# An attention and MoE kernel on one core: the order of its instructions taken from a table in place of a list scheduler

## The chip, the core and the metric

The kernel runs on one core of a Trainium2 chip. The metric is device time in microseconds (us) of one execution. The engines are named as in the profile: PE is TensorE, PEld its weight loads, DVE is VectorE, ACT ScalarE, POOL GpSimd and SP SyncE, which issues nearly all DMAs. Each engine works through its own list of instructions in the order in which the program emits them and waits on semaphores for the others.

## The reference

The inputs are q, k and v of 4 batches, 8 heads, 576 positions and 64 elements a head, a memory per head (M_prev, z_prev), a gate per head and four MoE weights. All is fp32.

```python
scores = scale * np.matmul(q, k.transpose(0, 1, 3, 2))       # causal mask, softmax over keys
local = np.matmul(a, v)
q_p = phi(q)                                                 # elu(q) + 1
mem_out = (q_p @ M_prev) / (q_p @ z_prev + 1e-06)            # per head
attn = g * mem_out + (1 - g) * local                         # g = sigmoid(beta)
x = attn.transpose(0, 2, 1, 3).reshape(2304, 512)
h = np.maximum(np.maximum(x @ w1, x @ w2), x @ w3)           # 512 -> 768
out = h @ w_out                                              # 768 -> 512
```

## The kernel before

**Tiling.** The 576 positions are cut in two halves of 320 and 256 (HALVES). The work of attention is done in 32 pairs: half by half, batch by batch, two heads at a time (`pairs`). For one pair the kernel loads q, k and v, builds phi(q) on ACT, DVE and POOL, brings q and k into transposed form, takes the scores (`scores_top`, `scores_both`, `scores`: bank bs), masks them and takes the row minimum on DVE, the exponential on ACT and the scaling on POOL. The scaled phi(q) lies in the same buffer p as the probabilities, so that one product with [M_prev; v] gives the gated sum (`values`: bank bv). P is transposed on PE (bank bt) for pairs 0 to 9, and from pair 10 by DVE and two DMAs (`turn_h`, `turn_p`, `move_h`, `move_p`, tiles dh, dp and pt). The result goes as a high and a low part (xh, xl) into SBUF.

**MoE.** When the four pairs of a batch and half are done, their x is one group of 320 or 256 rows; there are eight groups. A group has 18 pieces of 12 matmuls (`moe_up`: 4 slices of 128 inputs, 3 products of high and low parts each, fp32r) and two or three of 18 or 36 (`moe_down`), all in the banks bm. The slices of one piece need the x of one pair each, so the first three matmuls of group 0 can run when pair 0 is done and the last three when pair 3 is. Until all weights are in, the pieces have only bank bm0, for the other two serve the decoding of weights: 24 chunks, each loaded by SP, widened by ACT and DVE and split by ACT and POOL or DVE (`load_weights`); six chunks are decoded early, then one with each piece.

**The plan.** Nothing is emitted while this program runs. `Plan` (L94) notes each operation with its regions of SBUF and PSUM and so with what it depends on (`note`). A copy may have two forms, ACT or DVE, and a subtraction of a low part two, DVE or POOL (`copy`, `combine`). `emit` starts from ranks in order of noting, some of them set later (`P.late`), and shakes them with 156 seeds (`shaken`). `run` (L353) then is a list scheduler with costs per operation, delays between engines (`AFTER`), 250 ns more for a PE instruction that waits for another engine (`SLACK`) and a simple model of DMA; it picks the form that ends first and emits the ready operation of lowest rank on the engine that is free first. For a change between PE's tile shapes (128 by 128, 64 rows, 64 columns) it adds time. All planned instructions are emitted on one line, L452.

**Fillers.** Until the first operation that writes bank bm0, `run` emits on PE a matmul of zeros into bm0 (L416) wherever its plan has a gap. These are the fillers:

```python
if e == "pe" and filler:
    while when - free[e] > (FILL_GAP if free[e] < WARM else FILL_WARM):
        if real:
            self.nc.tensor.matmul(**filler)
        free[e] += 107 if free[e] < WARM else 54
```

Of the kernel before, what the change touches and what calls it, by code (L numbers as in the profile page):

```python
# [12 lines left out]
F32 = mybir.dt.float32  # L13
# [12 lines left out]
class Half:  # L26

# [24 lines left out]

FILL_GAP, FILL_WARM, FILL_FROM, WARM = 60, 80, 450, 7500


NEAR = 1

SEEDS = (
# [18 lines left out]
)  # L82

BANK = (((0, 512),),)


class Op:
    __slots__ = (
        "eng", "cost", "fn", "args", "prio", "num", "deps", "users", "left", "move", "at", "end", "can",
        "more",  # L90
    )


class Plan:  # L94

    ENGINES = {"pe": "tensor", "dve": "vector", "act": "scalar", "pool": "gpsimd", "sp": "sync"}

    AFTER = {
        "pe": {"pe": 0, "dve": 200, "act": 200, "pool": 200, "sp": 190},
        "dve": {"pe": 235, "dve": 130, "act": 130, "pool": 205, "sp": 120},
        "act": {"pe": 200, "dve": 145, "act": 130, "pool": 160, "sp": 145},
        "pool": {"pe": 200, "dve": 115, "act": 220, "pool": 100, "sp": 70},
        "sp": {"pe": 2800, "dve": 2800, "act": 2800, "pool": 2800, "sp": 2800},
    }  # L110


    PEN = {"dve": 300}

    SLACK = 250

    def __init__(self, nc):
        self.nc = nc
        self.ops = []
        self.seen = {}  # L120
        self.filler = None
        self.kept = set()
        self.tied = []
        self.late = 0

    @staticmethod
    def region(ap):

        if ap.space == bass.MemoryType.DRAM:
            last = sum(st * (n - 1) for st, n in ap.ap)  # L130
            return 0, 1, ((ap.offset, ap.offset + last + 1),)
        row = ap.ap[0][0]
        dims = sorted(
            ((abs(st), n) for st, n in ap.ap[1:] if n > 1 and st and st % row), reverse=True
        )
        p0, f0 = divmod(ap.offset, row)
        p1 = p0 + ap.ap[0][1] + sum(st // row * (n - 1) for st, n in ap.ap[1:] if st % row == 0)
        size = 1
        while dims and dims[-1][0] <= max(size, 4):
            st, n = dims.pop()  # L140
            size += (n - 1) * st
        runs = [f0]
        for st, n in dims:
            runs = [r + i * st for r in runs for i in range(n)]
        return p0, p1, tuple((r, r + size) for r in runs)

    @staticmethod
    def meet(a, b):
        return (
            a[0] < b[1] and b[0] < a[1]  # L150
            and any(r0 < t1 and t0 < r1 for r0, r1 in a[2] for t0, t1 in b[2])
        )

    @staticmethod
    def covers(a, b):
        return (
            a[0] <= b[0] and b[1] <= a[1]
            and all(any(r0 <= t0 and t1 <= r1 for r0, r1 in a[2]) for t0, t1 in b[2])
        )
# [25 lines left out]
    def cost(self, eng, name, kw):  # L185
        out = kw["out"]
        n = 1
        for d in out.shape[1:]:
            n *= d
        if name == "dma_start":  # L190
            return {80: 680, 64: 715}.get(out.shape[0], 510)
        if eng == "pe":
            if name == "transpose":
                return 2.5 + 0.837 * kw["in_"].shape[0]
            if kw["rhs"].dtype != F32:
                return 13.3 + n / 2.4
            if self.mode(name, kw)[0] == 64:
                return 106 + 1.67 * n if out.shape[0] > 64 else 115
            return 1.69 * n
        psum = any(  # L200
            isinstance(a, bass.AP) and a.space == PSUM for a in kw.values()
        )
        if eng == "dve":
            if name == "reciprocal":
                return 75 + 6.25 * max(0, n - 1)
            if name in ("tensor_scalar", "tensor_copy") and not psum:
                return 68 + 0.52 * n
            if name == "tensor_reduce":
                n = 1
                for d in kw["in_"].shape[1:]:  # L210
                    n *= d
            if name == "tensor_tensor_reduce":
                return 76 + 1.042 * n + 62 * isinstance(kw["scalar"], bass.AP)
            return 68 + 1.042 * n
        if eng == "act":
            c = (51 if psum else 93) + 0.833 * n
            if out.space == PSUM:
                c += 80
            if len(out.shape) == 3 and out.ap[-1][0] > 1 and psum:
                c += 190  # L220
            return c + 93 * sum(isinstance(kw.get(a), bass.AP) for a in ("bias", "accum_out"))
        if eng == "pool":
            if name == "tensor_tensor":
                a = kw["in0"]
                apart = out.offset // out.ap[0][0] != a.offset // a.ap[0][0]
                return 142 + 2.13 * n + 140 * apart
            if name == "tensor_scalar":
                return 310 + 0.87 * n
            return 100 + 1.1 * n
        raise ValueError(eng)  # L230

    @staticmethod
    def mode(name, kw):

        w = kw["in_" if name == "transpose" else "lhsT"]
        rows = 64 if w.shape[0] <= 64 else 128
        if name == "transpose" or w.dtype != F32:
            return rows, 128
        return rows, 64 if w.shape[-1] <= 64 else 128

    @staticmethod
    def move(*aps):

        piece, size = 4096, 4
        for d in aps[0].shape:
            size *= d
        for ap in aps:
            run = 4
            for st, n in reversed(ap.ap if ap.space == bass.MemoryType.DRAM else ap.ap[1:]):
                if 4 * st != run:  # L250
                    break
                run *= n
            piece = min(piece, run)
        many = any(st == 0 for ap in aps for st, n in ap.ap[:1])
        if aps[0].shape[0] == 32 and piece > 1024:
            return size / piece * (31 + 0.0475 * piece) / 16
        return size / piece * (125 if many else 9.7 + 0.0435 * piece) / 16

    @classmethod
    def tiling(cls, eng, name, kw):  # L260

        if eng != "pe":
            return None, None, 0
        w = kw["in_" if name == "transpose" else "lhsT"]
        mode = cls.mode(name, kw)
        if mode == (128, 64):
            return mode, kw["out"].offset // kw["out"].ap[0][0] // 64, 0
        return mode, w.offset // w.ap[0][0] // 64, w.shape[-1]

    @staticmethod  # L270
    def shares(eng, name, kw):

        if eng == "pool":
            return True
        if eng != "dve":
            return False
        aps = [a for a in kw.values() if isinstance(a, bass.AP) and a.shape[-1] > 1]
        inputs = [a for k, a in kw.items() if k in ("in_", "in0", "in1") and a.space != PSUM]
        if len(inputs) > 1:
            return True  # L280
# [5 lines left out]
    def note(self, can):  # L286
# [12 lines left out]
        if after is not None:  # L299
            ins += after if isinstance(after, list) else [after]  # L300
# [1139 lines left out]
```

## Time and profile before

| | us |
|---|---|
| median of 3 runs | 481.31 (481.14 to 483.03) |
| profiled execution, first to last instruction | 478.1 (its whole time is not given apart from this) |
| PE busy | 468.6 |
| DVE, POOL, ACT busy | 345.0, 296.8, 279.7 |

The busy time of an engine is the time covered by its instructions. Matmuls are pipelined and overlap, so their durations are longer than the distance from one start to the next; where a cost is read, the starts are compared. The profile shows an fp32 matmul of less than the full array as two instructions. In the rows below "x" is a count, and in square brackets stands the idle time of the engine before an instruction and what ended it.

### The profile page before, as it was taken

The page shows a single profiled execution, that of the slowest core. Times are in us where ns is not written, and L with a number is a line of the kernel's source. Part 1 is how long each engine was busy: PE and PEld are TensorE (multiplying, and loading weights), DVE is VectorE, ACT ScalarE, POOL GpSimd, SP SyncE. Part 2 cuts the span into 40 slices and gives each one's busy share as a digit, 9 for nine tenths or more (in the row PEclk, how much of TensorE's full clock was granted, in tenths as well). Part 3 has the DMA queues.
Part 4 walks back from the last instruction along what each step waited for, and adds up shares of the span by engine and source line. Part 5 has one row for each costly group of instructions (what it writes and reads, how often), then busy time and mean ns, then how long its engine had stood idle before and what let it go on. Part 6 is the DMA issues. An engine that isn't in the chain of part 4 may idle for free.

```text
span 478.1 us, 10593 instructions
## 1 busy us (share of the span) xinstructions
PE 468.6 (98%) x3387; PEld 407.7 (85%) x3387; DVE 345.0 (72%) x1127; ACT 279.7 (59%) x784; POOL 296.8 (62%) x452
## 2 busy tenths in 40 slices
PE   9989999999999999999999999999999999999996
PEld 7654778787999889998999888997999888988995
DVE  3788999997689967687688766887779676630230
ACT  5588987886668563565556655746566565422111
POOL 3866797977878866476558864876776776511000
PEclk9998999999999999999999999999999999999999
DMA  5788888765558978777999999999997887674001
GB/s 124 179 221 262 231 223 241 235 164 127 128 122 220 252 172 224 176 185 232 262 215 236 258 260 252 239 209 260 267 268 201 219 244 198 198 198 111 23 0 46
DMA packets 147256, 94.24 MB, mean 197 GB/s; under 512 B 99968, under 2 KB 126848, under 8 KB 147200
## 3 DMA queue, kind: packets, MB, share of 16 engines
q1 hardware_dynamic: 146384, 93.36, 74.4%
q8 instruction: 27, 0.44, 0.4%
q10 hardware_dynamic: 816, 0.20, 0.2%
q14 instruction: 29, 0.24, 0.2%
HBM read 61.94 MB, written 31.59 MB: 196 GB/s over the span
## 4 chain that ended last, share of the span: by engine, by line
PE 91%; DMA 4%; SPq 2%; ACT 1%; issue 0%; DVE 0%; ACTq 0%
PE bm L452 64%; PE bv L452 11%; PE bs L452 10%; PE bt L452 4%; DMA rw<-in_moe_w_dram 4%; PE bm L416 2%; SPq L452 2%; DMA rk<-in_q_dram 1%; ACT p L452 0%; ACT k L452 0%; ACT rk L452 0%; ACT t L452 0%; DVE bm L452 0%; DVE p L452 0%; ACT bm L452 0%
## 5 line engine op out<-in xcount | busy, mean ns | idle before, releaser
L452 PE MATMUL bm<-xh,wh 128*128 128x320 f32 (+1 forms) x576 | 170.6, 302 | 0.5 <-DVE xh L452 0.3
L452 PE MATMUL bm<-xl,wh 128*128 128x320 f32 (+1 forms) x576 | 169.3, 299 | 0.0
L452 PE MATMUL bm<-xh,wl 128*128 128x320 f32 (+1 forms) x576 | 168.0, 297 | 0.0
L452 POOL TENSOR_SCALAR p<-p,sum,gb 128x320 f32<-128x320 f32 (+3 forms) x128 | 89.4, 703 | 38.8 <-DVE sum L452 27.0
L452 PEld LDWEIGHTS bm<-xh,wh 128*128 128x128 f32 x576 | 108.1, 190 | 3.6 <-ACT t L452 0.9
L452 PEld LDWEIGHTS bm<-xl,wh 128*128 128x128 f32 x576 | 108.6, 190 | 1.2 <-issue 0.3
L452 PEld LDWEIGHTS bm<-xh,wl 128*128 128x128 f32 x576 | 108.4, 189 | 1.2 <-issue 0.8
L452 ACT ACTIVATE p<-p,st 128x320 f32<-128x320 f32 (+4 forms) x144 | 84.2, 585 | 42.2 <-DVE st L452 39.9
L452 DVE TENSOR_TENSOR t<-bm,t 128x320 f32<-128x320 f32 (+1 forms) x96 | 43.1, 449 | 49.6 <-PE bm L452 42.0
L452 DVE CUSTOM_DVE_ANT_0 p<-bs,mask 128x320 f32<-128x320 f32 (+3 forms) x128 | 59.1, 470 | 15.3 <-PE bs L452 14.9
L452 PE MATMUL bs<-k,qs 128*128 128x288 f32 (+5 forms) x264 | 59.4, 311 | 0.0
L452 DVE STREAM_TRANSPOSE rk<-p 128x512 f32<-128x512 f32 (+1 forms) x80 | 55.7, 720 | 2.4 <-POOL p L452 2.1
L452 POOL TENSOR_TENSOR p<-phf,nn 128x128 f32<-128x128 f32 (+1 forms) x96 | 37.4, 396 | 15.6 <-DVE rk L452 6.9
L452 PEld LDWEIGHTS bs<-k,qs 128*128 128x128 f32 (+1 forms) x264 | 42.0, 186 | 3.6 <-issue 1.7
L452 PE MATMUL bv<-pt,rv 128*64 128x256 f32 (+1 forms) x384 | 42.9, 348 | 0.0
L452 POOL TENSOR_TENSOR xl<-kt,xh 128x256 fp32r<-128x256 f32 (+1 forms) x28 | 22.6, 808 | 31.9 <-ACT kt L452 31.3
L452 PEld LDWEIGHTS bv<-pt,rv 128*64 128x64 f32 x384 | 29.4, 139 | 15.2 <-issue 0.8
L452 PE MATMUL bm<-woh,hl 128*128 128x512 f32 (+1 forms) x102 | 39.0, 384 | 0.0
L452 PE MATMUL bm<-woh,hh 128*128 128x512 f32 (+1 forms) x102 | 38.8, 384 | 0.0
L452 PE MATMUL bm<-wol,hh 128*128 128x512 f32 (+1 forms) x102 | 38.6, 380 | 0.0
L452 ACT COPY t<-bm 128x256 f32<-128x256 f32 (+1 forms) x45 | 17.8, 395 | 29.7 <-PE bm L452 25.5
L452 ACT CAST hh<-t 128x256 fp32r<-128x256 f32 x44 | 17.7, 402 | 29.8 <-DVE t L452 29.8
(102 smaller groups left out, 839.7 us busy)
## 6 DMA issues: line engine op xcount, KB each, us to landing
dp<-rk SPq DMA_DIRECT2D x16, 1024.0 KB, 5.2
pt<-dp SPq DMA_DIRECT2D x64, 256.0 KB, 5.0
rw<-in_moe_w_dram SPq DMA_DIRECT2D x18, 512.0 KB, 5.0
dh<-rk SPq DMA_DIRECT2D x6, 704.0 KB, 4.4
pt<-dh SPq DMA_DIRECT2D x24, 176.0 KB, 3.7
rw<-dq SPq DMA_DIRECT2D x32, 128.0 KB, 5.9
rv<-in_v_dram SPq DMA_DIRECT2D x32, 128.0 KB, 3.1
out_dram<-g SPq DMA_DIRECT2D x15, 256.0 KB, 2.9
```

Of the source, the lines that this page charges most:

```text
L416: self.nc.tensor.matmul(**filler)
L452: getattr(getattr(self.nc, self.ENGINES[e]), name)(**kw)
```

## The change

The list scheduler, its costs, its dependency tracking and the seeds are removed. `note` keeps the forms of each operation in program order. `emit` reads a table of 5431 words. A word is the position of the next operation among those not yet emitted, counted in program order; a "b" takes its second form (DVE for a copy, POOL for a subtraction), and "+n" puts n fillers on PE ahead of it. The thirteen words with "+" hold 119 fillers, the last at word 193, and 205 words have a "b". What each operation computes, its tiles and its buffers are the same. The `late` and `tied` marks, which only the scheduler read, are gone from the functions that set them.

```diff
-from heapq import heappop, heappush
-from random import Random
...
-FILL_GAP, FILL_WARM, FILL_FROM, WARM = 60, 80, 450, 7500
...
-SEEDS = (
-    834900, 908918, 588425, 647536, 878120, 41042, 332167, 847884, 614213, 478334,
...
+ORDER = """
+    2 0 1 0 0 0 2 15 15 15 4 3 2 1 21+30 22+12 21 21 0 17 15 140 82 10 79 78 77 13 76 6 12 12 18+9 17 17 9 0
+    19+10 0 27 0 17 8 6 23 0 16 39+12 5 20 15 34 34 51 33 13 7 34 34 1 0 15 6 2 28 16+6 8 5 5 24 6 2 20 1 0 9
+    9 9 31+16 0 8 2 1 3 21 25 106 11+4 1 23 4 9 4 26+2 38 38 8b 1 65 3 23 10 3 1 8 19 7 19 4+6 0 5 3 28 28 50
+    8 1 10 2 10 0 31 17 65 14 14 21 63 27 4 4 3 11 57 22 15 23+8 21 30 50 21 143 21 15 11 19 19b 2 21 20 13 18
+    39 21 5 2 129 11 11 2 16 17 3 3 5 11 1 11 9 14+1 6 13b 13 0 9 1 109 108 7 18 27 7b 25 8 100 24 0 0 5 21 39
...
+    3b 18 3 7 1b 0 0 13 13 13 0 0 0 0 0 0 0 0 0 0 0 0b 0 0 0 0 0 0 0 0 0 0 0 0 0 0 0 2 2 2 2 2 2 2 0 0 0 0 0 0
+    0 8 0 0 0 0 0 0 0 0 0 0 0 0 0 0 0 0 0 0 0 0 0 0 0 0 0 0 0
+"""
...
     def note(self, can):
-        op = Op()
-        after = can[0][2].pop("after", None)
-        op.can = [(e, name, kw, self.cost(e, name, kw)) for e, name, kw in can]
-        op.eng = op.can[0][0] if len(can) == 1 else None
-        op.more = {e: (self.shares(e, n, kw), *self.tiling(e, n, kw)) for e, n, kw in can}
-        op.prio, op.users, op.end = len(self.ops) + self.late, [], None
...
+        for _, _, kw in can:
+            kw.pop("after", None)
+        self.ops.append(can)
 
     def emit(self):
-        ops = self.ops
-        prio = [o.prio for o in ops]
-        for seed in SEEDS:
-            prio = self.shaken(prio, seed)
-        return self.run(prio, True)
...
-    def run(self, prio, real):
...
-            if e == "pe" and filler:
-                free[e] = max(free[e], FILL_FROM)
-                while when - free[e] > (FILL_GAP if free[e] < WARM else FILL_WARM):
-                    if real:
-                        self.nc.tensor.matmul(**filler)
-                    free[e] += 107 if free[e] < WARM else 54
...
-        return max(free.values())
+        rest = deque(self.ops)
+        ahead = []
+        for word in ORDER.split():
+            word, _, fill = word.partition("+")
+            for _ in range(int(fill or 0)):
+                self.nc.tensor.matmul(**self.filler)
+            at = int(word.rstrip("b"))
+            while len(ahead) <= at:
+                ahead.append(rest.popleft())
+            eng, name, kw = ahead.pop(at)[word.endswith("b")]
+            getattr(getattr(self.nc, self.ENGINES[eng]), name)(**kw)
+        assert not rest and not ahead
...
-    LATE, MOE_LATE = 100, 100
-    FAR, MV = 60, 2
+    MV = 2
...
-    KEEP_LATE = 60
...
-            P.late = LATE
...
-            if e:
-                P.tied.append(len(P.ops))
```

## Rows read from the trace of the kernel before

**Rows 1.** The page: busy time by engine, and granted PE clock in 40 slices.

```profile
PE 468.6 (98%) x3387; PEld 407.7 (85%) x3387; DVE 345.0 (72%) x1127; ACT 279.7 (59%) x784; POOL 296.8 (62%) x452
...
PEclk9998999999999999999999999999999999999999
```

**Rows 2.** Busy time by stage: stretch, length, five engines, clock, DMA share, GB/s.

```profile
0.00:24.00 24.00, 22.86 (x245) 17.87 (x246) 14.19 (x61) 13.29 (x42) 14.61 (x37) 1.00 0.64 152
24.00:51.00 27.00, 22.82 (x164) 14.01 (x164) 23.90 (x89) 22.56 (x65) 18.62 (x34) 0.94 0.86 243
51.00:100.00 49.00, 48.94 (x333) 40.03 (x331) 46.84 (x129) 42.07 (x114) 39.02 (x56) 1.00 0.78 227
100.00:260.00 160.00, 160.00 (x1084) 144.53 (x1083) 127.48 (x416) 98.56 (x287) 111.58 (x169) 1.00 0.77 194
260.00:440.00 180.00, 179.94 (x1306) 158.38 (x1306) 125.04 (x419) 95.95 (x261) 112.25 (x158) 1.00 0.88 228
440.00:474.10 34.10, 34.10 (x268) 32.91 (x264) 7.55 (x18) 6.90 (x17) 0.74 (x1) 1.00 0.06 20
474.10:478.10 4.00, 0.00 (x0) 0.00 (x0) 0.00 (x0) 0.38 (x1) 0.00 (x0) 0.83 0.11 35
```

**Rows 3.** Timeline of PE, 0 to 51 us: start, length, instruction, idle before.

```profile
0.99 2.95 PE L416 MATMUL bm<-mask 128*128 128x128 bf16 x26 [0.99 <-DVE mask L683]
...
9.86 1.95 PE L416 MATMUL bm<-mask 128*128 128x128 bf16 x32
...
24.72 0.52 PE L452 MATMUL bt<-ident,p 128*128 128x128 f32 x3 [0.42 <-POOL p L452]
...
26.23 0.49 PE L452 MATMUL bt<-ident,rk 80*128 80x80 f32 x4 [0.55 <-ACT pt L452]
...
29.62 1.01 PE L416 MATMUL bm<-mask 128*128 128x128 bf16 x15
30.45 0.40 PE L452 MATMUL bm<-xh,wh 128*128 128x320 f32 x1
...
34.86 0.43 PE L452 MATMUL bt<-ident,rk 80*128 80x80 f32 x3 [1.31 <-ACT pt L452]
...
44.14 0.29 PE L452 MATMUL bt<-ident,rk 80*128 80x80 f32 x1 [0.75 <-ACT pt L452]
...
48.94 0.74 PE L452 MATMUL bt<-ident,p 128*128 128x128 f32 x5 [0.81 <-ACT pt L452]
```

**Rows 4.** Busy time by stretch again, within the second stage.

```profile
36.40:39.80 3.40, 3.40 (x16) 1.50 (x15) 1.98 (x9) 3.33 (x9) 1.64 (x4) 0.50 0.67 213
39.80:51.00 11.20, 9.30 (x67) 5.66 (x66) 10.71 (x38) 9.32 (x28) 9.12 (x17) 1.00 0.94 270
```

**Rows 5.** Groups by shape: the fillers (busy us, mean ns, idle before).

```profile
L416 PE MATMUL bm<-mask 128*128 128x128 bf16 x185 | 15.3, 238 | 1.0 <-DVE mask L683 1.0
```

**Rows 6.** Timeline of PE around a 64-row block and the last bv block.

```profile
58.62 0.41 PE L452 MATMUL bm<-xh,wh 128*128 128x320 f32 x1
58.87 0.30 PE L452 MATMUL bm<-xl,wh 128*128 128x320 f32 x1
...
437.82 0.39 PE L452 MATMUL bm<-woh,hh 128*128 128x512 f32 x1
438.14 0.65 PE L452 MATMUL bv<-pt,mv 128*64 128x256 f32 x4
...
440.23 0.50 PE L452 MATMUL bm<-woh,hl 128*128 128x512 f32 x1
440.57 0.39 PE L452 MATMUL bm<-wol,hh 128*128 128x512 f32 x1
```

**Rows 7.** Groups by shape: the same subtraction on DVE and on POOL.

```profile
L452 DVE TENSOR_TENSOR hl<-t,hh 128x256 fp32r<-128x256 f32 x20 | 11.3, 564 | 5.0 <-ACT hh L452 4.5
...
L452 POOL TENSOR_TENSOR hl<-t,hh 128x256 fp32r<-128x256 f32 x28 | 21.3, 762 | 9.3 <-ACT hh L452 8.2 <-ACT hhr L452 0.4 <-DVE sum L452 0.2
```

**Rows 8.** The chain that ended last: start, length, what.

```profile
440.30 33.81 PE bm L452 x262
```

**Rows 9.** DMA issues: count, KB each, median us to landing.

```profile
pt<-dp SPq DMA_DIRECT2D x64, 256.0 KB, 5.0
```

More of the change, by code (lines that the diff above doesn't have):

```diff
@@ L113 @@
-    PEN = {"dve": 300}
-    SLACK = 250
     def __init__(self, nc):
@@ L119, in __init__ @@
         self.ops = []
-        self.seen = {}
         self.filler = None
[L122 to L159, printed above, removed]
     def __getattr__(self, eng):
@@ L183, in combine @@
         self.note([(e, "tensor_tensor", dict(out=out, in0=in0, in1=in1, op=op)) for e in engines])
[L185 to L280, printed above, removed]
-        return (
-            name in ("tensor_scalar", "tensor_copy")
-            and bool(aps) and not any(a.space == PSUM for a in aps)
-        )
@@ L286, in note @@
-    def note(self, can):
-        op = Op()
-        after = can[0][2].pop("after", None)
-        op.can = [(e, name, kw, self.cost(e, name, kw)) for e, name, kw in can]
-        op.eng = op.can[0][0] if len(can) == 1 else None
-        op.more = {e: (self.shares(e, n, kw), *self.tiling(e, n, kw)) for e, n, kw in can}
-        op.prio, op.users, op.end = len(self.ops) + self.late, [], None
-        kw = can[0][2]
-        op.move = self.move(kw["out"], kw["in_"]) if can[0][1] == "dma_start" else 0
-        op.deps = {}
-        outs = [kw[k] for k in ("out", "accum_out") if kw.get(k) is not None]
-        ins = [a for k, a in kw.items() if k not in ("out", "accum_out") and isinstance(a, bass.AP)]
-        if after is not None:
-            ins += after if isinstance(after, list) else [after]
-        for aps, write in ((ins, False), (outs, True)):
-            for ap in aps:
-                if ap.space == bass.MemoryType.DRAM and ap.tensor.name not in self.kept:
-                    continue
-                here, psum = self.region(ap), ap.space == PSUM
-                keep = []
-                for e in self.seen.get(ap.tensor.name, ()):
-                    there, w, o = e
-                    other = op.eng is None or o.eng != op.eng
-                    if psum and other and self.meet(here[:2] + BANK, there[:2] + BANK):
-                        op.deps[o] = True
-                    elif (write or w) and self.meet(here, there):
-                        if o is not op:
-                            op.deps[o] = True
-                        if write and self.covers(here, there):
-                            continue
-                    keep.append(e)
-                keep.append((here, write, op))
-                self.seen[ap.tensor.name] = keep
-        op.deps.pop(op, None)
-        op.left = len(op.deps)
-        op.num = len(self.ops)
-        for o in op.deps:
-            o.users.append(op)
-        self.ops.append(op)
-        return op
@@ L328, in emit @@
-    def emit(self):
-        ops = self.ops
-        prio = [o.prio for o in ops]
-        for seed in SEEDS:
-            prio = self.shaken(prio, seed)
-        return self.run(prio, True)
-    def shaken(self, prio, seed):
-        rng = Random(seed)
-        n = len(prio)
-        size = rng.choice((5, 20, 60, 250, 1000, n))
-        lo = rng.randrange(max(1, n - size)) if seed % 4 == 0 else rng.randrange(max(1, 2400 - size // 2))
-        mag = rng.choice((2, 6, 15, 40, 100))
-        share = rng.choice((0, 0, 0.05, 0.3, 1.0))
-        move = 0 if share else rng.gauss(0, mag)
-        out = list(prio)
-        for i in range(lo, min(n, lo + size)):
-            out[i] += move
-            if rng.random() < share:
-                out[i] += rng.gauss(0, mag)
-        for i in self.tied:
-            out[i] = out[i - 1] + 1e-6
-        return out
@@ L567, in attention_memory_moe @@
     P = Plan(nc)
-    P.kept |= {t[:].tensor.name for t in r_dp.tiles + r_dh.tiles + r_dq.tiles + [dz, dk]}
     rw = tile_([128, 3072], U32, "rw")
@@ L768, in phi @@
         r = raw[pi]
-        P.late = 30
         c = len(HALVES[hi].blocks)
@@ L802, in phi @@
         r["f"] = fv, rv
-        P.late = 0
     def phi_to_p(pi, e):
```

256 lines of the change are left out of this document (137 added, 119 removed), and 23 rows, old and new, of tables (ORDER, SEEDS).

## The prediction

> **What bounds the kernel now.** I read the page's first two parts first: TensorE (PE) is busy 98% of the 478.1 us span, the next engine, VectorE (DVE), 72% [rows 1]. That says which engine, not where time can be had, so the second view is the busy time by stage [rows 2]. Five stages matter. Up to 24 us PE is busy 22.86 of 24, but much of it is not work: fillers (matmuls of zeros into bm's first bank, line 416). From 24 to 51 us it has gaps, 22.82 of 27. From 51 to 440 us it is busy in every microsecond but 0.12 (0.06 each in two rows). From 440.3 a single run of 262 MoE matmuls ends the work in 33.8 us [rows 8], and 4 us of copy and store follow. So the end is set by PE: the moment from which its queue never empties (51 us), plus the work left then, plus the 4 us. An order can move three things: how much of 0 to 51 us is lost, how many costly turns the dense part holds, and whether that part stays dense.
>
> The profiled execution is known by its span, 478.1 us. The three timed runs have a median of 481.31; I carry the 3.2 us between them over unchanged and give the forecast against 481.31.
>
> **What the head holds.** The timeline of PE alone [rows 3] shows 185 fillers [rows 5] in the first 30.4 us, from 0.99 to the last run of 15 at 29.62; the first MoE matmul is at 30.45 and ends them by rule. Waits begin at 24.7: 0.42, 0.55, 1.31, 0.75 and 0.81 us in the five rows, 3.84 us together, the first for a normalized p, the others for a copy that frees bank bt. The granted clock is 0.50, so 1.2 instead of 2.4 GHz, in the 3.4 us from 36.4 [rows 4], some 6 us after the last filler and 1.5 us after the wait of 1.31 us has ended. PE is busy there, so 1.7 us are lost.
>
> **The change, part by part.**
>
> *Nothing is computed otherwise.* The table has 5431 words, and the trace has 5431 planned instructions when each fp32 matmul that shows as two is counted once. So PE's work is the same but for fillers, and every gain or loss is place. 205 words take the second of two engines; from the groups by shape I count 165 such choices before (122 subtractions on POOL, 43 copies on DVE; the hl rows are the pattern, 28 on POOL, 20 on DVE [rows 7]). The 40 more move about 762 - 564 = 0.2 us each onto the slower engine if they are subtractions, and take 0.56 us each from DVE. After 51 us no engine but PE sets the end and POOL is busy 262.85 of 389 us [rows 2], so I cost this at nothing; cover gone, a subtraction that feeds a PE operand is late by that 0.2 us, 8 us if all 40 are.
>
> *A. Fillers.* The thirteen words with a plus carry 119 fillers, 66 fewer. In the run of 32 at 9.86 [rows 3] one takes (1.95 - 0.24) / 31 = 55 ns, so 66 x 0.055 = 3.6 us. A filler stands where the plan expects PE to wait, so fewer of them mean either less waiting or an earlier first MoE matmul, after which gaps stay bare. The last plus stands at word 193. Before the 193rd planned instruction of the old trace (22.9 us, counted in the timeline) there were 161 fillers: 42 more than 119 at the same amount of issued work, 2.3 us, which I take as head that is really shorter. The other 24 (1.3 us, at 24.1, 25.1 and 29.6) go to the second reading; I take half. A = -2.3 - 0.65 = -2.95. Bounds: 0 (the waits stay, only not padded) and -3.6.
>
> *B. Waits and clock from 24 to 51 us.* 3.84 us of waits and 1.7 us of half rate are the most that can go, -5.5. On the other side, DVE is busy 23.90 of these 27 us, ACT 22.56, the DMA engines 86% [rows 2]: this stretch holds the chain of the first four batch-0 head pairs, with weight decoding beside it, and no order takes more than DVE's 3.1 us of idle out of it without moving decoding later. And it can get worse: bare gaps where fillers were may bring another half-rate stretch, +1.7. I take -1.0, nearer to the small end, since the search may push decoding out of the head but DVE has 2.2 us spare of the 49 that follow.
>
> *C. Turns in the dense part.* PE pays when it goes from full 128x128 tiles to 64-wide or 64-row ones and back. The last bv block [rows 6]: 437.82 to 438.14 is 0.32 us where a 512-column matmul beside it takes 0.23, and after it 440.23 to 440.57 is 0.34: 0.09 in and 0.11 out, 0.2 us. After a block of 64-row bs matmuls, 58.62 to 58.87 is 0.25 where a 320-column matmul takes 0.147, 0.1 out. There are 32 bv blocks (one a pair) and at least as many bs ones before pair 10; two that touch save one such 0.2 us. Bounds: -6.4 (all 32 bv blocks find a neighbour) and +2 (ten blocks more). The plan before already priced the turns once an order was found but chose by rank; moving single instructions can join blocks directly. I take six joined, -1.2.
>
> *D. The dense part.* It has no wait to lose, so an order can only harm it: each engine still runs its own queue in order, and a PE instruction whose operand is late holds the whole MoE stream behind it. The moved DMAs count here: SP's queue issues all pt<-dp loads (64, 5.0 us to land each [rows 9]) and the weight loads in the new order. Bounds 0 and +6 (worked out below); I take +0.7, three or four waits of the 0.2 us size.
>
> *E. The end.* The last group's up and down matmuls need the last pair's values; 33.8 + 4.0 us stay. 0.
>
> Sum: -2.95 - 1.0 - 1.2 + 0.7 = -4.45; 481.31 - 4.45 = 476.9 us, 0.9% faster. Its own range is 473.0 (A whole, half of B's 5.5, ten blocks joined: 3.6 + 2.75 + 2.0) to 478.4 (A alone).
>
> **The rivals.**
>
> *1. The head is as long as before.* Its end is set by DVE and the DMA engines and not by PE, so removed fillers are bare waits. For it: DVE 23.90 of 27 us, DMA 0.86 [rows 2]. Against: 42 fewer fillers before 22.9 us, where DVE is busy only 14.19 of 24. C and D then nearly cancel: 481.31 - 1.2 + 0.7 = 480.8.
>
> *2. The clock falls more.* With fillers gone from about word 193 on, the half-rate stretch comes twice more: +3.4 against A's -2.95, and with C and D the time is 481.3. For it: in the old trace the fall came 6 us after the last filler, with no wait before it longer than 1.31 us. Against: once MoE matmuls are there, they fill gaps as well. The Trainium skill, TensorE: Matmul & The Clock Gate, section Why this matters for your kernels, has the rule that idle gaps between bursts of matmuls send the array to half rate, and asks for short ones only. The trace bears the rule out only in part: it shows a fall with no gap longer than 1.31 us; if only long gaps counted, bare short ones would cost nothing here, and by the row a fall costs 1.7 us.
>
> *3. Slower: the table spends the slack of late operands.* A fixed list by a plan's times starts PE instructions with less margin than the removed plan's SLACK of 250 ns. 22 pairs (10 to 31) get P back by DMA, pt<-dh or pt<-dp; a bv block that waits for its last load stops PE with everything behind it. The price is the wait per pair: at 0.24 us x 22 = 5.2 us the gain of A to C is gone, and that is the point from which it decides; at 0.4 us it is 8.8 - 5.15 = +3.6, 485. For it: the loads land 5.0 us after issue, with DMA engines 88% busy from 260 to 440 us [rows 2, 9]. Against: today not one recorded wait stands in that stretch, and the MoE work that covers it is as large as before.
>
> *4. Deeper.* The head loses A's full 3.6 and 3 of B, and half of the bv blocks are joined, -3.2: 481.3 - 9.8 = 471.5. For it: these losses are all in the trace. Against: each needs the better end at once.
>
> That the table does the same as the plan before is excluded by its counts, 119 and 205.
>
> **How the numbers follow.** The forecast has 0.50, the deeper case 0.17, rivals 1 and 2 together 0.18, slower 0.15. The range from 470.5 to 483 leaves out about half of the slow rival and the far end of the deep one. About 0.5% (2.4 us) is what a measurement of this kernel can tell from no change: faster is below 478.9, the forecast and the deep case, 0.67; same up to 483.7, 0.18; slower 0.15.
>
> **What would show it.** A: some 119 fillers on line 416, and the bv blocks of the first pairs (19.5 to 46 us now) 2 to 3 us earlier. B: the moment from which PE has no wait lies at 46 to 49 us instead of 51, and the half-rate stretch is absent or not longer than 3.4 us. C: fewer first-after-block intervals of 0.25 to 0.34 us. D: no more than a microsecond of waits on PE after 51 us. The prediction is wrong if that moment stays at 51 us, if waits for pt stand in the dense part, or if the end moves by something other than the head and the turns.

## The result, and the profile after

The changed kernel takes 477.99 us (median of 7 runs, 477.13 to 479.77) and the kernel before, on the same chip, 482.06 us (7 runs, 479.88 to 485.01): a ratio of 0.991, with an interval of 0.988 to 0.994. The prediction was 476.9 us, faster. Sign and size came out. Two of its terms did not: the head gained 6.4 us where the forecast's A and B add up to 3.95, and the dense part lost some 6 us where 0.7 was forecast. That the sum still fits is luck, as the last part works out.

The page of the changed kernel, its first two parts:

```profile
span 476.2 us, 10470 instructions
...
PE 464.3 (98%) x3321; PEld 402.7 (85%) x3321; DVE 369.1 (78%) x1205; ACT 256.7 (54%) x725; POOL 280.5 (59%) x433
...
PEclk9999999999999999999999999999999999999999
```

Against [rows 1], PE has 66 instructions fewer (185 - 119 fillers), the half-rate stretch is absent, and the other engines have traded places: DVE is 24.1 us busier, ACT 23.0 and POOL 16.3 us less. The windows by stage (columns as in [rows 2]) say where that matters:

```profile
0.00:24.00 24.00, 21.39 (x210) 15.94 (x211) 14.69 (x68) 16.01 (x48) 14.17 (x36) 1.00 0.69 174
24.00:51.00 27.00, 25.27 (x175) 16.59 (x176) 25.32 (x91) 25.17 (x77) 22.14 (x37) 1.00 0.88 243
51.00:100.00 49.00, 48.24 (x330) 38.93 (x327) 46.85 (x138) 40.40 (x111) 37.32 (x56) 1.00 0.81 225
100.00:260.00 160.00, 156.42 (x1046) 140.88 (x1045) 139.30 (x447) 87.06 (x252) 99.20 (x155) 1.00 0.75 190
260.00:440.00 180.00, 179.82 (x1312) 158.17 (x1311) 134.03 (x443) 85.03 (x233) 104.74 (x148) 1.00 0.87 230
440.00:474.10 34.10, 33.16 (x260) 32.20 (x258) 8.88 (x23) 3.04 (x8) 2.94 (x4) 1.00 0.04 12
```

From 24 to 51 us PE works 2.45 us more than before, and DVE, ACT and POOL all do (POOL 3.5 us more). From 100 to 260 us it is the other way round: PE was busy for all 160 us, and is now idle for 3.58 of them, while DVE goes from 127.48 to 139.30. The waits of PE (columns: engine, tile and line waited for, then us in total, times, longest) name what it lacks:

```profile
PE bs L259 <- DVE st L259: 3.6, 7, 1.1
PE bt L259 <- ACT pt L259: 1.6, 4, 0.8
PE bt L259 <- ACT p L259: 1.3, 1, 1.3
...
PE bs L259 <- DVE k L259: 0.6, 1, 0.6
```

The lines for pt and p are the head's. Six of the seven waits for st, 3.0 us, and the one for k lie between 100 and 260 us. Here is the longest of them, the timeline of all engines around 222 us:

```profile
219.51 1.44 POOL L259 TENSOR_TENSOR qs<-rw,qs 128x256 fp32r<-128x256 f32 x2 [0.22 <-DMA mv<-in_v_dram]
...
220.31 1.25 DVE L259 TENSOR_TENSOR qs<-rw,qs 128x256 fp32r<-128x256 f32 x2
...
220.69 0.40 PE L259 MATMUL bm<-woh,hh 128*128 128x512 f32 x1
...
220.93 0.39 PE L259 MATMUL bm<-woh,hl 128*128 128x512 f32 x1
...
221.48 0.41 DVE L259 TENSOR_TENSOR hl<-t,hh 128x256 fp32r<-128x256 f32 x1
221.82 0.45 DVE L259 CUSTOM_DVE_ANT_0 p<-bs,mask 128x288 f32<-128x288 f32 x1
...
222.19 0.08 DVE L259 DVE_READ_ACCUMULATOR2_ANT st<- 128x1 f32 x1
222.31 0.52 DVE L259 CUSTOM_DVE_ANT_0 p<-bs,mask,st 128x288 f32<-128x288 f32 x1
222.41 0.44 PE L259 MATMUL bs<-k,qs 128*128 128x448 f32 x1 [1.10 <-DVE st L259]
```

The matmul at 222.41 needs a free score bank bs; there are two. Two mask operations on DVE read one bank each. The first frees the bank that is needed: it ends with its read-out at 222.27, and PE starts while the second is still running. In DVE's queue three subtractions (qs twice, hl once, 1.25 and 0.41 us) stand ahead of the masks. All three have a POOL form; the first and the last are among those that the table took from POOL, the middle one was on DVE before. The first of them is long besides, about 0.9 us where the next, of the same shape, takes 0.41: until 220.95 a subtraction of POOL runs beside it. PE's next MoE matmuls stand behind the matmul that waits.

To follow the gain through the run I add up the work of PE without fillers (each shape at its median start-to-start interval) and ask how much earlier the changed kernel has done the same amount: its lead. A median stands for every interval of a shape, so a value is good to about 1 us. In the head the blocks themselves can be read: the first bv block of pairs 0 to 4 started at 19.5, 27.8, 37.0, 46.0 and 57.0 us and now starts at 19.1, 25.2, 32.2, 39.6 and 50.6, so the lead grows to 6.4 us. After that it shrinks: 6.2 us at 100, 3.8 at 160, 0.1 at 260, and then it stays within a microsecond, 0.9 at 460. The last matmul ends 0.9 us earlier (473.2 instead of 474.1). The span is 1.9 us shorter: the other 1.0 us lies behind the last matmul, where copy and store took 4.0 us in that execution of the kernel before and 3.0 here. In the traces of all twelve experiments that follow they take 3.0 to 3.4 us, also where the end has the old order, so this microsecond is not the table's.

That this pair of spans differs by 1.9 us and the medians by 4.1 comes at least in part from the clock. Over 68 executions of the kernel before, taken beside the experiments, the mean granted clock is 0.9937 and the span follows it (correlation -0.77): nine executions at 0.998 or more have a median of 478.0 us, eleven below 0.9915 have 481.8. Clock is not all of it: those nine still range from 477.0 to 479.9. The profiled one, 478.1, was among the quicker. The changed kernel's thirteen executions have a mean clock of 0.9985 and a median span of 476.3. So about 2 us of the gain is there at full clock (478.0 to about 476), and the other half, nearly 2 us, is half-rate time of which the changed kernel has less. Two things stay open. The profiled execution of the kernel before lost 1.7 us to its half-rate stretch, so at full clock it would have taken some 476.4 us; why the full-clock executions take 478.0 no trace shows, for none of them was profiled. And the changed head is not free of the fall: 4 of its thirteen executions have a mean clock of 0.996, one of the seven beside the result and three of the six of e8_as_changed. Of the 42 executions of six variants below with the same head (e5_less_dve, e7_new_to_120, e9 to e12) 28 are below 0.998.

### The profile page after: what moved, and what is told of

Read it like the earlier page. It is cut to its first block, busy times and chain, and to the rows that moved or that the text cites. A ratio compares the mean times of both kernels' runs of the same rounds, so it can differ in the third digit from the quotient of the medians.

```text
span 476.2 us, 10470 instructions
## 1 busy us (share of the span) xinstructions
PE 464.3 (98%) x3321; PEld 402.7 (85%) x3321; DVE 369.1 (78%) x1205; ACT 256.7 (54%) x725; POOL 280.5 (59%) x433
## 5 line engine op out<-in xcount | busy, mean ns | idle before, releaser
L259 PE MATMUL bm<-xh,wh 128*128 128x320 f32 (+1 forms) x576 | 167.1, 305 | 0.3 <-DVE t L259 0.3
L259 PE MATMUL bm<-xl,wh 128*128 128x320 f32 (+1 forms) x576 | 165.8, 298 | 0.0
L259 PE MATMUL bm<-xh,wl 128*128 128x320 f32 (+1 forms) x576 | 162.3, 297 | 0.0
L259 POOL TENSOR_SCALAR p<-p,sum,gb 128x576 f32<-128x576 f32 (+3 forms) x128 | 87.3, 687 | 63.4 <-DVE sum L259 49.5
L259 DVE TENSOR_TENSOR t<-bm,t 128x320 f32<-128x320 f32 (+1 forms) x96 | 43.4, 453 | 39.1 <-PE bm L259 24.1
L259 DVE CUSTOM_DVE_ANT_0 p<-bs,mask 128x192 f32<-128x192 f32 (+3 forms) x128 | 59.6, 474 | 15.9 <-PE bs L259 14.6
L259 PE MATMUL bs<-k,qs 128*128 128x288 f32 (+5 forms) x264 | 67.1, 312 | 3.6 <-DVE st L259 3.0
L259 DVE STREAM_TRANSPOSE rk<-p 128x512 f32<-128x512 f32 (+2 forms) x80 | 57.6, 729 | 5.1 <-POOL p L259 4.8
L259 POOL TENSOR_TENSOR p<-phf,nn 128x128 f32<-128x128 f32 (+1 forms) x96 | 36.7, 390 | 20.3 <-DVE nn L259 14.6
L259 PE MATMUL bv<-pt,rv 128*64 128x256 f32 (+1 forms) x384 | 40.4, 344 | 0.0
L259 POOL TENSOR_TENSOR phe<-phf,z 128x384 f32<-128x384 f32 (+1 forms) x32 | 28.9, 902 | 16.0 <-DVE phf L259 5.7
L259 POOL TENSOR_TENSOR xl<-kt,xh 128x256 fp32r<-128x256 f32 (+1 forms) x28 | 22.4, 803 | 23.1 <-ACT kt L259 23.1
L259 ACT COPY t<-bm 128x320 f32<-128x320 f32 (+1 forms) x38 | 15.3, 402 | 30.8 <-PE bm L259 21.4
```

What stands on the lines that cost most here:

```text
L259: getattr(getattr(self.nc, self.ENGINES[eng]), name)(**kw)
```

## The experiments

The question was where the lead of 6 us goes between 100 and 260 us. One theory: the table's own later part loses it, by what it puts on DVE ahead of the operations that PE waits for. Its rival: a lead can't be kept there, whatever the order, because with the head packed tighter the work that follows comes due before its operands. Later the first was split: is it DVE's total load, or single instructions at the wrong place in its queue? The lead at five moments, for all runs that bear on it:

| run | 100 us | 160 | 260 | 400 | 460 |
|---|---|---|---|---|---|
| changed kernel | 6.2 | 3.8 | 0.1 | 0.4 | 0.9 |
| e1_new_head | 4.0 | 2.0 | 2.0 | 1.6 | 1.6 |
| e2_old_head | -0.8 | -2.2 | -6.6 | -6.5 | -5.7 |
| e3_old_forms | 4.3 | 2.1 | 0.6 | -5.5 | -6.3 |
| e6_new_to_150 | 7.0 | -0.2 | -0.2 | -0.2 | -0.2 |
| e7_new_to_120 | 5.8 | 3.8 | 3.6 | 2.9 | 2.9 |
| e5_less_dve | 6.8 | 6.1 | 3.8 | 4.4 | 4.7 |
| e9_copies_back | 4.9 | 4.1 | 1.3 | 0.8 | 1.4 |
| e10_subs_back | 6.6 | 5.3 | 5.2 | 5.5 | 5.9 |
| e11_less_dve_far | 5.8 | 5.0 | 2.7 | -1.7 | -1.2 |
| e12_subs_far | 4.9 | 3.7 | 3.6 | 3.5 | 3.4 |

**Head and rest apart.** Two mixed orders, each a legal order of the same instructions, and the changed kernel's order with the engines of before.

```diff
 # e1_new_head
-    all 5431 instructions as the table has them
+    the table's first 1000; then the others in the order and with the engines of the kernel before
 # e2_old_head
+    the kernel before's first 1000 (with its fillers); then the others as the table has them
 # e3_old_forms
+    the table's order; each instruction on the engine that the kernel before gave it (208 words differ)
```

> The first 1000 of the 5431 instructions (up to about 90 us) in the new order and with the new choices of engine, all others in the order and with the engines of the kernel before. In the changed kernel the work of PE is 6.6 us ahead of the kernel before at 50 us and still 5.8 us at 120 us, and level at 260 us, with 3.4 us of waits for DVE between 127 and 223 us. Theory 1 (the gain is the head's, and the later part of the new table gives it back by its own order or its own choice of engines): the lead is kept, 475.5 to 477 us against 482.06 before, PE busy at least 159 of 160 us from 100 to 260 us. Rival (the lead is lost to supply: attention's chain on DVE, ACT and POOL can't feed a PE that is 6 us further, whatever the order): waits of PE for DVE return between 100 and 260 us, and the time is 478 to 480 us, no better than the changed kernel.

Measured: 477.82 us against 481.13, ratio 0.995 (0.992 to 0.998), between the two times expected. Its lead is lost at two single waits and kept from 160 us to the end. So a lead can be kept: the old dense order carries 1.6 to 2 us through 300 us. The first wait stands at the joint, which neither kernel has. The second lies over 50 us behind it, and whether it comes from the joint or from the old order with a lead is not shown here, which leaves the rival half alive for the stretch up to 144 us. The two waits (timeline of PE):

```profile
93.24 0.41 PE L254 MATMUL bt<-ident,p 128*128 128x128 f32 x2 [1.72 <-ACT pt L254]
...
143.99 0.42 PE L254 MATMUL bm<-xh,wh 128*128 128x320 f32 x1 [1.71 <-DVE sum L254]
```

> The first 1000 instructions as in the kernel before, fillers included, all others in the new order with the new engines. Theory 1: nothing is gained in the head, and the new later part loses up to the 5.8 us that it loses in the changed kernel: 483 to 487 us against 482.06, with waits of PE for DVE between 100 and 260 us. Rival (loss by supply alone): with no lead there is nothing to lose, 481 to 482.5 us and almost no wait of PE after 51 us.

Measured: 485.48 us, ratio 1.010 (1.006 to 1.014). Without any lead to lose, the later part of the table still loses 5.8 us between 100 and 260 us, with the same waits of PE as the changed kernel (for st, 3.0 us in 6) and the same load of DVE, its windows row:

```profile
100.00:260.00 160.00, 156.43 (x1044) 139.12 (x1043) 139.09 (x450) 90.82 (x264) 97.90 (x153) 1.00 0.72 182
```

So the loss belongs to that stretch of the table itself, and the rival falls.

> The new order and its 119 fillers throughout, but each copy and each subtraction on the engine that it had before (165 second choices in place of 205; 59 copies go back from DVE to ACT and 19 subtractions from DVE to POOL, net). Theory 2 (the lead goes because DVE, 139 of 160 us busy from 100 to 260 us against 127 before, releases the score banks late): DVE falls back to some 127 us there, PE's waits for DVE go below 1 us, and the time is 474.5 to 476.5 us if the head keeps its lead. Rival (the order of the later part, not the engines, puts the scores too close together): the waits stay at 3 us or more and the time is 477 to 480 us. A head that needs the new engines would show as a lead under 5 us at 50 us.

Measured: 485.6 us, ratio 1.011 (1.007 to 1.014). DVE is back at 126.92 us in the stretch and the waits for st fall to 1.0 us in 2, but others come (for t of ACT and of DVE, 2.4 us each in the whole run), and PE is busy only 174.00 of the 180 us from 260 to 440. Neither of the two times expected came. From 100 to 260 us the lead falls by 3.7 us with less load on DVE; the rest of the loss comes later. The old engines as a whole don't suit the new order:

```profile
260.00:440.00 180.00, 174.00 (x1262) 152.40 (x1262) 120.87 (x406) 92.81 (x258) 110.10 (x156) 1.00 0.85 224
```

**The fillers.**

```diff
 # e4_no_fill: the thirteen words with a plus
-    ... 21+30 22+12 ... 18+9 ... 19+10 ...
+    ... 21 22 ... 18 ... 19 ...
 # e8_as_changed: the changed kernel once more
```

> The changed kernel without its 119 fillers. Theory (fillers only keep the clock up, the head's end is set by the chain over DVE, ACT, POOL and the DMAs): the granted clock is at 1.2 GHz for some of the first 30 us, the transposes and scores there take twice as long and sit on that chain, 1 to 4 us slower than the changed kernel (479 to 482 us). Rival (the fillers themselves cost time, since they stand in PE's queue ahead of work): 476 to 477.9 us, faster by up to 1.5 us. Third: PE is never on the chain of the head, within 0.5 us of 478 us.

> The changed kernel itself, as the measure for the other three on this chip: 478 us within 1, 0.991 of the kernel before. The theory on the clock (half of the gain is half-rate time that the kernel before has in most of its executions): its executions have a mean granted clock of 0.999 to 1.0 throughout, those of the kernel before beside it 0.987 to 1.0, and the spans of the latter fall on a line of some 400 to 480 us per unit of missing clock, with 477 to 478 us at full clock.

Measured: 478.46 us without fillers, 478.47 with them (on two chips; ratios to the kernel before beside each 0.995 and 0.993, 0.993 to 0.997 and 0.991 to 0.995). PE runs its first 18 us slowly without them and then stands where the changed kernel stands. Its timeline of PE has, for the block of four 64-row bs matmuls that takes 0.80 to 0.81 us in the changed kernel:

```profile
10.22 1.44 PE L259 MATMUL bs<-rk 64*128 64x192 f32 x4
...
12.88 1.43 PE L259 MATMUL bs<-rk 64*128 64x320 f32 x4
```

The granted clock does not show this slowness, it reads 1.00 over these 18 us (windows row):

```profile
0.00:18.00 18.00, 12.26 (x49) 7.32 (x49) 9.48 (x46) 10.29 (x30) 10.17 (x27) 1.00 0.67 170
```

So the third outcome named for e4_no_fill came: to leave the fillers out does not move the time, and in this kernel they are only a mark of where the plan expected PE to wait. Of what was expected of e8_as_changed, the time came out, the clock in part: three of its six executions are at 0.996, and the spans of the kernel before fall on a line of some 350 us per unit of missing clock, not 400 to 480.

**Where the new order should stop.**

```diff
 # e6_new_to_150 / e7_new_to_120
+    the table's first 1800 / first 1400; then the others in the order and with the engines of before
```

> The first 1800 instructions (to about 150 us) as in the table, the rest in the order and with the engines of the kernel before. The old order lost nothing from 160 us on when it was 2 us ahead. Theory 1 (the later part of the table is worse than the old order by itself): with some 5 us of lead at the joint and up to 2 us lost there, 3 to 5 us are left at 260 us and at the end: 474 to 476 us where the changed kernel takes 478. Rival (a lead over 2 us can't be fed): a long wait of PE at or soon after the joint, lead 2 us, 477 to 478 us as with the joint at 90 us.

> The same with the joint at 1400 instructions, about 120 us. It tells where the lead goes when the old order takes over: the joint at 90 us lost 2 us at the joint and 1.7 us in one wait for DVE at 144 us. If that second wait belongs to the old order with a lead of more than 2 us, it is here too (lead 2 us after 145 us, 477 us); if it came from the joint, the lead stays at 4 us or more and the time is 474 to 476 us.

Measured: e6 480.63 us, ratio 0.998 (0.996 to 1.000); e7 475.61 us, 0.986 (0.984 to 0.989). The joints make the difference. e7 loses 1.8 us between 120 and 144 us, 0.58 of it in a wait at the same MoE matmul at which e1_new_head waited 1.71, so the old order with a lead has a part in that wait; then it holds 3 to 4 us to the end. At e6's joint PE waits once, and runs at about half clock (granted 0.54) after it (timeline of PE, then the window behind the wait):

```profile
151.84 0.80 PE L255 MATMUL bm<-woh,hh 128*128 128x512 f32 x1 [4.43 <-ACT t L255]
```

```profile
151.80:155.50 3.70, 3.66 (x10) 2.95 (x10) 1.30 (x3) 0.49 (x2) 3.54 (x7) 0.54 0.83 208
```

A 512-column MoE matmul starts every 0.42 us in that window instead of every 0.23. That one wait and its slow stretch eat a lead of 6 us, and neither of the times expected came; what the old order does with such a lead this run can't say.

**DVE's load by itself.** The order is the changed kernel's to the last instruction; only the engine of single instructions between no. 1180 and no. 3079 (about 95 to 260 us) is given back, where the kernel before had them elsewhere.

```diff
 # e10_subs_back: 30 subtractions from DVE to POOL
-    ... 56 ... 53 ... 40 ... 175 ... 80 ...
+    ... 56b ... 53b ... 40b ... 175b ... 80b ...
 # e9_copies_back: 32 copies from DVE to ACT
-    ... 48b ... 37b ... 74b ... 32b ...
+    ... 48 ... 37 ... 74 ... 32 ...
 # e5_less_dve: both, 62 words
```

> The changed kernel, but of the instructions tabled as number 1180 to 3079 (about 100 to 260 us) the 62 that the table newly puts on DVE are back where they were, 32 copies on ACT and 30 subtractions on POOL; all else as in the table. In the changed kernel PE's lead over the kernel before falls there from 5.9 to 0 us, in steps at waits for DVE of 0.3 to 1.1 us. Theory 2 (DVE's load is the cause): DVE falls from 139 to about 110 of the 160 us, the waits for DVE mostly go, at least 3 us of the lead stay, and the time is 3 us or more under the changed kernel's (473 to 475.5). Rival (the order between scores and their readers is the cause, and the engines were chosen to fit it): new waits for ACT or POOL take the place of those for DVE, and the time is within 1 us of the changed kernel's or above it.

> Of the 62 instructions that went back from DVE between 100 and 260 us and brought 3.2 us, only the 32 copies, to ACT. Theory 2a (DVE's load as a sum is what counts): DVE falls from 139 to about 125 us of 160, about half of the gain comes, 476.5 to 477.3 us where the changed kernel takes 478.5. Rival 2b (single instructions ahead of the score masks count; before the longest wait, 1.1 us at 222 us, DVE runs two subtractions of 0.6 us each and one of 0.4): the copies bring under 0.8 us, 477.7 us or more.

> The other part alone: the 30 subtractions back to POOL, the copies as tabled. Theory 2a: about half of the 3.2 us, 476.3 to 477.3. Rival 2b: most of it, 475.2 to 476.2 us, and the wait of 1.1 us gone.

Measured: both 475.25 us, ratio 0.986 (0.984 to 0.989); the copies alone 476.67, 0.991 (0.988 to 0.993); the subtractions alone 474.07, 0.985 (0.983 to 0.988), the lowest ratio of all kernels run. Against the changed kernel as e8_as_changed has it (0.993, 0.991 to 0.995) both together and the subtractions stand clear; the copies alone do not, and the subtractions alone are not clear of both together. The windows row from 100 to 260 us, of e5_less_dve, e9_copies_back and e10_subs_back:

```profile
100.00:260.00 160.00, 158.97 (x1069) 143.91 (x1068) 116.86 (x394) 99.98 (x291) 118.66 (x186) 1.00 0.77 198
```

```profile
100.00:260.00 160.00, 158.29 (x1060) 143.02 (x1059) 129.48 (x421) 98.69 (x291) 100.37 (x156) 1.00 0.77 194
```

```profile
100.00:260.00 160.00, 159.52 (x1080) 145.21 (x1080) 127.76 (x431) 91.73 (x262) 120.48 (x189) 1.00 0.78 199
```

PE's waits in that stretch of e10_subs_back:

```profile
PE bs L259 <- DVE st L259: 0.5, 1, 0.5
```

The first theory holds: what the table puts on DVE loses most of the lead. PE's order is the same in all these kernels, so each of its starts can be set beside the same start in the changed kernel. From 100 to 260 us e10_subs_back wins 4.7 us, and 4.3 of them come at seven matmuls: 0.50 each at 151.7 and 155.1 us, 0.72 each at 176.6 and 200.3, 1.25 at 222.4, 0.24 at 232.4, 0.33 at 246.2. Six of these are the waits for st and k of the changed kernel; the seventh of those, at 127.1, stays, and is the 0.5 us of the row above.

Whether it is DVE's load or single places in its queue is not settled as cleanly. e5_less_dve takes 22.4 us off DVE in this stretch, e9_copies_back 9.8 and e10_subs_back 11.5, and they win 3.0, 2.4 and 4.7 us against the changed kernel. So the total is not the measure: twice the relief won less. But the copies alone also end the waits at 200.3 and 222.4 us, though none of them stands in the 2.5 us of DVE's queue ahead of these, and their time, 476.67 us, is the one that the theory of the sum expected; that of the subtractions lies below what either expected. Whatever leaves DVE early enough lets it reach the mask sooner. What tells the two kinds apart is the other engine: in all three kernels with copies back on ACT PE starts late by 0.3 us more at 191.6 and by 0.6 to 0.7 at 261.7, and in neither of the two with subtractions alone. For the wait at 222.4 the queue shows which subtractions delayed the mask; for the waits at 151.7 and 155.1 none of the 30 stands in the 2.5 us ahead, and how their delay is handed on was not followed. To move only the subtractions right ahead of a mask was not tried.

Measured by starts, the late starts of PE from 100 to 260 us (over 0.12 us beyond the shape's median interval in the two kernels) add up to 1.5 us in the kernel before, 6.2 in the changed one, 3.4 in e5_less_dve and 1.9 in e10_subs_back. A wait row counts from a modelled end and so shows less than PE loses.

**The same to the end of the table.**

```diff
 # e11_less_dve_far: 123 words, no. 1180 to the end (72 copies to ACT, 51 subtractions to POOL)
 # e12_subs_far: the 51 subtractions alone
```

> As with the 62 instructions back, and also those that the table newly puts on DVE after number 3080, 123 in all. After 260 us DVE is busy 132 of 180 us, PE waits for nothing and the lead stays at 4.3 to 4.7 us. Theory 2 (a lead is lost only where DVE is late): nothing to win there, 475.3 us within 0.7. Rival (any return to the old engines helps): 474 us or less. Third (the later order is built on the new engines): new waits of PE after 260 us, 477 us or more.

> The changed kernel with all 51 subtractions that the table newly puts on DVE after number 1180 back on POOL, to the end, and all copies as tabled. With copies and subtractions back after 3080 as well, 481.1 us was taken, and PE waited after 260 us for ACT (t, g, pt; about 3 us) and for POOL (p, xl; 1.5 us). If the loss there is the copies' (ACT), this takes 474 to 475 us like the kernel with the 30 subtractions of the middle stretch alone (474.1). If it is the subtractions' (POOL is busy 118 of 180 us there), waits for POOL stand after 260 us and the time is 477 us or more.

Measured: e11 481.06 us, ratio 0.999 (0.997 to 1.001); e12 475.01, 0.986 (0.984 to 0.988). e11 loses 4.7 us against the changed kernel after 260 us and e12, without the copies, 1.0, so most of what the rest had won goes to the copies given back to ACT there. The windows row of e11_less_dve_far, and its waits from 260 to 440 us:

```profile
260.00:440.00 180.00, 175.79 (x1275) 154.04 (x1275) 112.19 (x384) 92.12 (x255) 118.22 (x169) 1.00 0.85 225
```

```profile
PE bm L259 <- ACT t L259: 1.6, 2, 1.4
PE bs L259 <- POOL p L259: 0.8, 1, 0.8
PE bm L259 <- ACT g L259: 0.8, 1, 0.8
PE bm L259 <- POOL xl L259: 0.7, 1, 0.7
```

The longest is for t, which ACT makes for the MoE matmuls; right ahead of it in ACT's queue stands one of the copies given back, 0.40 us, and another ahead of g. The waits for p and xl are POOL's, and the one for xl is there in e12 too. For the copies the table was right there. e12 keeps its lead from 260 us on (3.6 to 3.4).

## Why the prediction came out, point by point

**The profiled execution and what lies around it.** The 3.2 us that I carried over between span and median are not constant. The time outside of the span is 1.8 us (477.99 - 476.2, and the same in every run); the rest belongs to the execution that happened to be profiled, its clock in part.

**A, the head before 24 us: right, with the wrong object.** Pair 1's bv block starts 2.6 us earlier, where A said 2.95 and its first reading 2.3. The count of fillers was a good sign of a shorter head, with some luck in the figure: 161 stand before 22.9 us by time, but only 149 before that word in the order of the old kernel's program, and 30 instead of 42 would have made 1.65 us. e4_no_fill shows that the fillers are no cost. Rival 1, a head as long as before, falls with the earlier blocks.

**B, 24 to 51 us: right in kind, undersized.** I took -1.0 of at most -5.5; the lead grew from 2.6 us (pair 1) to 6.4 (pair 4), so about -3.8, of which 1.7 is the missing half-rate stretch. I had limited the rest by DVE's 3.1 us of idle, and that bound held: waits of PE in that stretch fell from 3.84 to 1.6 us, by 2.2. What was too small was the value taken within the bound. DVE did go from 23.90 to 25.32 of 27 us, and the decoding was not moved out: 11 weight loads are issued by 51 us instead of 8, the first of them as the 22nd instruction instead of the 143rd. An idle share of 12% on the busiest engine beside PE was slack that an order could take out, within the chain of pairs and not by moving work away.

**C, turns: right.** Counted in the timelines of PE, 157 changes of tile shape became 146; behind 51 us, where C looked, 103 became 89. That is seven blocks joined, about -1.4 at the forecast's own 0.2 us, for its -1.2. No run tried the turns by themselves.

**D, the dense part: the sign right, the size wrong.** +0.7 was said; the lead falls by some 6 us between 100 and 260 us, all of D's bound of +6, which the prediction calls worked out but nowhere works out. The step that failed stands earlier, where I costed the second choices at nothing: I took the 40 more for subtractions moved onto POOL, and looked for the cover in POOL's idle time. Compared one by one, 89 copies went from ACT to DVE and 30 back, 54 subtractions from POOL to DVE and 35 to POOL: a net of 59 copies and 19 subtractions onto DVE. The count of words with a b hides this, because for a copy the second choice is DVE and for a subtraction it is POOL. The cost came through the queue of DVE: the 30 subtractions of e10_subs_back take 0.2 to 1.2 us each there, and delay what stands behind them, masks that free a score bank above all. e10_subs_back gives the price by itself: 0.985 instead of 0.993 of the kernel before, so 0.8% or 3.7 us for 30 instructions. Rival 3 had the right kind of mechanism, lost slack before a PE operand, at the wrong place: no wait for pt from a DMA appeared in the changed kernel after 51 us. My sign for D, "no more than a microsecond of waits on PE after 51 us", was broken: 3.6 us of waits in one stretch.

**E, the end: right for PE.** The chain of the changed kernel ends as [rows 8] did, with 33.8 us of MoE matmuls; the 4.0 us behind them were no fixed cost, but 3.0 here:

```profile
437.32 2.10 PE bv L259 x20
439.41 33.76 PE bm L259 x263
```

**The clock, rival 2.** It did not come in the changed kernel's profile, though a wait of 1.26 us stands at 18.26. In five of its variants with the same head it did (e7, e9, e10, e11, e12), each time behind a wait of the same transposes near 31 us: e10_subs_back's timeline of PE has it, and behind it a stretch at 1.2 GHz, with PE busy all the time:

```profile
31.36 0.93 PE L259 MATMUL bt<-ident,rk 80*128 80x80 f32 x6 [1.50 <-DMA rk<-in_k_dram]
```

```profile
32.40:35.90 3.50, 3.50 (x19) 1.95 (x18) 2.74 (x9) 2.69 (x9) 1.34 (x4) 0.51 0.72 184
```

The waits there are 1.34 to 1.64 us in these five and 1.06 or less in the profiles of the new head without the fall. e9_copies_back has 6.8 us of it after its 1.34, the others 3.4. Before the waits PE had been doing thin work, transposes and 64-row blocks. As the programs are the same up to there, it is the execution that decides how long the wait is. The rule of the Trainium skill, TensorE: Matmul & The Clock Gate, section Why this matters for your kernels, that idle gaps bring half rate, is borne out by these and by e6's 4.43 us, but not by the length of a wait alone: 1.31 to 1.64 us in thin work were followed by it, in e2_old_head (at 0.50 from 36.7 us) only 0.80 us stood shortly before it and 1.84 us ten microseconds earlier, and e1_new_head's 1.72 and 1.71 us at 93 and 144 us were followed by full clock (1.00 in the 3.5 us behind each). Why the kernel before falls in 59 of 68 executions, mostly to 0.993 or less, and the changed one in 4 of thirteen, to 0.996, was not tried by an edit of its own; that its waits of 24 to 51 us are what does it rests on the correlation and these profiles alone.

**The sum.** 4.45 us were predicted, about 4.1 measured, and that they agree is luck. In the profiled pair PE gains 0.9 us: 6.4 in the head, where A and B say 3.95, less some 6 in the dense part, where C and D together say a gain of 0.5, and a little back behind it. The other 1.0 us of the spans' 1.9 is the tail of one execution, which the forecast had at 0. The remaining 2.2 us of the measured gain lie between the profiled execution of the kernel before and its median, half-rate time in part, and the forecast did not have them either: it carried that gap over unchanged.

## What to carry to other kernels

When a change moves instructions between engines, count each kind of instruction by the engine it leaves and the one it joins; the total of moves says nothing, and an engine that is idle 13% of a stretch (DVE here, 139.30 of 160 us) still delays the bottleneck if work that nobody waits for stands in its queue ahead of the operation that frees a bank. An order found by search can be mended by hand: take the stretch where the lead is lost, read what the waiting matmul waits for and what stands ahead of that, and give such instructions to an engine that has room (here 30 words, 0.8% faster again, while copies given to ACT cost waits elsewhere). And before carrying the gap between one span and a median over, look at the granted clock of several executions.

## What the runs showed of the hardware

- Without the fillers PE took 1.44 instead of 0.80 us for a block in the first 18 us, while its granted clock read 1.00, and it cost the kernel nothing: 478.46 against 478.47 us.
- The same subtraction on DVE takes longer while POOL runs a two-operand operation beside it. In the changed kernel the 128x256 one into qs takes 0.42 us (median of nine) with none beside it and 0.79 (median of seven) with one beside it for over half of its time.
- A single wait of 1.3 to 1.6 us in thin work was followed by 3.4 to 6.8 us at 1.2 GHz in six profiles, one of 0.80 us in a seventh (e2_old_head), and one of 4.43 us in the middle of dense MoE matmuls by 3.4 us, while two of 1.7 us in dense work were not. Over 68 executions of one and the same kernel the mean clock ranges from 0.987 to 1.0 and the span from 477.0 to 483.4 us.
- A wait row understates what PE loses: at 222.41 the row says 1.10 us, while the matmul before it started at 220.93 and such a one is followed after 0.24 us (220.69 to 220.93), so PE lost 1.24.
